# Linear attention and a GELU layer: k and v of the first batches in longer runs, the first y with t outer, and q transposed by DMA

## The chip, the cores and the metric

The kernel runs on one core of one Trainium2 chip. Time is device time of one execution in microseconds (us); the kernel before has a median of 308.79 us over three runs (308.36 to 309.51). Engines are named as in the profile: PE (TensorE, matrix multiply), DVE (VectorE), ACT (ScalarE), POOL (GpSimd) and SP (SyncE, which here only issues DMAs). SBUF is the memory that engines and DMAs share, PSUM the one that PE writes.

## The reference

Two stages. Attention takes q, k, v of 8 batches x 8 heads x 576 positions x 64. The second stage is a two-layer perceptron over 4608 tokens of width 512, with 2048 hidden columns.

```python
q_s = exp(q - max(q, axis=-1));  q_s = q_s / (sum(q_s, axis=-1) + 1e-09)   # over the 64 features
k_s = exp(k - max(k, axis=2));   k_s = k_s / (sum(k_s, axis=2) + 1e-09)    # over the 576 positions
kv  = einsum('bhsd,bhse->bhde', k_s, v)
att = einsum('bhsd,bhde->bhse', q_s, kv)
x = att.transpose(0, 2, 1, 3).reshape(4608, 512)
h = x @ w_in                                   # 512 -> 2048
y = (0.5 * h * (1 + erf(h / sqrt(2)))) @ w_out # 2048 -> 512
```

All inputs and the output are 32-bit floats. Neither kernel subtracts the maxima, which the quotients do not need. The sum over positions does not depend on their order, so k and v may be laid on the partitions in any way in which they agree; the rows of q fix which output row is which.

## The kernel before, in words

Work goes in nine chunks of 512 token rows: chunk b is positions 0 to 511 of batch b (partition p holds positions 4p to 4p+3, index j), and chunk 8 collects the 64 left over positions of all eight batches. For the sums over k the left over positions are used with their own batch.

The front of a chunk is this. `load` (L96) brings q, k, v of one batch by DMAs on SP: 1024 B runs for the main 512 positions, 256 B runs for the rest (`load_rest`, L91). ACT takes exp of q and k (`exp_q`, `exp_k`), DVE casts v to bf16 beside a column of ones per pair of heads (`cast_v`, L141). `norm_q` (L151) sums exp(q) over the features on DVE, takes reciprocals, and multiplies on POOL (or half on POOL and half on DVE). `kv_step` (L178) multiplies exp(k) with [v, 1] for one or two pairs of heads; the ones give the column sums, and DVE (or DVE and ACT, with `split`) scales the two 64x64 diagonal blocks into `kvbd`, a 128x128 block-diagonal matrix whose other blocks were set to zero once. `tp_step` (L202) transposes normalized exp(q) on PE, eight 128x128 blocks per half, and DVE copies the half from PSUM to `qT`. `x_step` (L220) multiplies `kvbd` with `qT` for one pair of heads and copies the product to `xT`.

Then `h_phase` (L239) runs 16 tiles t of four matmuls each (64 matmuls), with ACT taking GELU of each tile into `g`; `y_phase` (L254) runs, for each of four row groups j, 16 matmuls over t, and DVE copies the result, which SP stores. PSUM has three tiles for h, two for y and three for the front.

The order of the work is written by hand: every engine takes its instructions in the order of the program text. A dictionary passed to `h_phase` or `y_phase` says after which tile or matmul a piece of the next chunk's front is put. For chunk 0 the front stands alone ahead of everything (L338 to L347); for chunk 1 it is partly in the first y and its end, `kv_chain(1)` (L369), stands alone after it. From chunk 3 on the front is spread: exps on ACT after the last GELU of an h phase, `dve_front` (normalization, casts of v) in the second row of the y phase, kv, transposes and x inside the next h phase (`back`, L391: kv after tiles 1 and 2, transposes after 4 and 5, x after 8 to 11).

The weights come as 32-bit floats through five staging tiles (`wst`), and are cast to bf16: the first part of w_in by ACT (L348), the rest by DVE. In SP's order stand the loads of batch 0, five parts of w_in, four of w_out, then batches 1 and 2. A load into a staging tile waits for the cast that frees the tile, and everything after it on SP waits with it.

`warm` (L325) issues matmuls on zeros; their product is not used.

Of the kernel before, what the change touches and what calls it, by code (L numbers as in the profile page):

```python
# [11 lines left out]
ALU = mybir.AluOpType  # L12
# [4 lines left out]
def kernel(  # L17
# [11 lines left out]

    nc = tc.nc  # L30
# [10 lines left out]
    PA = 2 * D + 2  # L41

# [19 lines left out]
    v_aug = [singles.tile([128, J, HP, PA], BF16, name=f"v_aug{i}") for i in range(2)]  # L62
# [5 lines left out]
    def setup_tiles():  # L68
        nc.vector.memset(scr, 0.0)  # L69
        for i in range(2):  # L70
            nc.vector.memset(v_aug[i][:, :, :, D:D + 1], 1.0)
            nc.vector.memset(vr_aug[i][0:R, :, D:D + 1], 1.0)
            nc.vector.memset(vr_aug[i][R:128], 0.0)
            nc.vector.memset(ek_r[i][R:128], 0.0)
        for b in range(B):
            nc.gpsimd.memset(kvbd[b], 0.0)
# [6 lines left out]
    def load_main(b, name, t, eng, parts=1):  # L83
        f = f32in.tile([128, H, J * D], FP32, tag=name + "f")
# [3 lines left out]
        for i in range(parts):  # L88
            eng.dma_start(out=f[:, i * n:(i + 1) * n, :], in_=src[:, i * n:(i + 1) * n, :])

    def load_rest(b, name, t, eng):  # L91
        r = f32in.tile([R, H, D], FP32, tag=name + "r")
        st[b][name + "r"] = r
        eng.dma_start(out=r, in_=t[b, :, M:S, :].rearrange("h p d -> p h d"))

    def load(b, qp=1, kp=1, vp=1, keng=None):  # L96
        keng = keng or nc.sync
        load_main(b, "q", q, nc.sync, qp)
        load_rest(b, "k", k, keng)
        load_main(b, "k", k, keng, kp)  # L100
        load_rest(b, "v", v, nc.sync)
        load_main(b, "v", v, nc.sync, vp)

    def load_qrest():
        f = f32in.tile([128, J, H, D], FP32, tag="qf")
# [7 lines left out]
    def exp_main(b, name, parts=1):  # L113
        e = attn_sb.tile([128, J, H, D], BF16, tag="e" + name)
# [18 lines left out]

    def cast_vr(b):
# [11 lines left out]
    def cast_v_all(b):  # L146
        cast_vr(b)
        for hp in range(HP):
            cast_v(b, hp)

    def norm_q(b, parts=1, engs=None):  # L151
        engs = engs or [nc.gpsimd]
        eq = st[b]["eq"]
        qsum = small.tile([128, J, H], FP32, tag="qsum")
        recq = small.tile([128, J, H], FP32, tag="recq")
        n = H // parts
        for i in range(parts):
            hs = slice(i * n, (i + 1) * n)
            nc.vector.reduce_sum(out=qsum[:, :, hs], in_=eq[:, :, hs, :], axis=AX.X)  # L159
            nc.vector.reciprocal(recq[:, :, hs], qsum[:, :, hs])  # L160
            engs[i % len(engs)].tensor_tensor(  # L161
                out=eq[:, :, hs, :], in0=eq[:, :, hs, :],
                in1=recq[:, :, hs].unsqueeze(3).to_broadcast([128, J, n, D]), op=ALU.mult,
            )
# [13 lines left out]
    def kv_step(b, hps, split=False):  # L178
# [8 lines left out]
        for hh in range(2):  # L187
# [3 lines left out]
            if split and hh == 1:  # L191
                for i in range(n):
                    nc.scalar.activation(  # L193
                        out=dst[:, i], in_=src[:, i], func=AF.Copy, scale=rec[pr, i:i + 1]
                    )
            else:
                nc.vector.tensor_tensor(  # L197
                    out=dst, in0=src, in1=rec[pr, 0:n].unsqueeze(2).to_broadcast([64, n, D]),
                    op=ALU.mult,
                )  # L200

    def tp_step(b, half, eng="v"):  # L202
        if half == 0:
            st[b]["qT"] = attn_sb.tile([128, J, HP, 128], BF16, tag="qT", name="qT")
        ps = psum_a.tile([128, J, 2, 128], BF16, tag="a")
        for i in range(2):
# [7 lines left out]
        o = st[b]["qT"][:, :, 2 * half:2 * half + 2, :]  # L214
        if eng == "v":
            nc.vector.tensor_copy(out=o, in_=ps)  # L216
        else:
            nc.scalar.copy(out=o, in_=ps)

    def x_step(b, hp, eng="v"):  # L220
        if hp == 0:
            st[b]["xT"] = attn_sb.tile([128, HP, M], BF16, tag="xT", name="xT")
        ps = psum_a.tile([128, M], FP32, tag="a")
        if b < B:
            nc.tensor.matmul(ps, kvbd[b][:, hp, :], st[b]["qT"][:, :, hp, :], start=True, stop=True)  # L225
        else:
            for bb in range(B):
# [5 lines left out]
                )  # L233
        if eng == "v":
# [4 lines left out]
    def h_phase(c, ins):  # L239
# [3 lines left out]
        for t in range(NDF):  # L243
            ps = psum_h.tile([128, M], FP32, tag="h")
            for dm in range(NDM):
                nc.tensor.matmul(  # L246
                    ps, wi_bf[:, dm, t * 128:(t + 1) * 128], xT[:, dm, :],
                    start=(dm == 0), stop=(dm == NDM - 1),
                )
            nc.scalar.activation(out=g[:, t, :], in_=ps, func=AF.Gelu)  # L250
            for f in ins.get(t, []):
                f()

    def y_phase(c, ins):  # L254
        g = st[c]["g"]
        for j in range(J):
            ps = psum_y.tile([128, DM], FP32, tag="y")
            for t in range(NDF):
                nc.tensor.matmul(  # L259
                    ps, g[:, t, j * 128:(j + 1) * 128], wo_bf[:, t, :],  # L260
                    start=(t == 0), stop=(t == NDF - 1),
                )
                for f in ins.get((j, t), []):
                    f()
            y_sb = moe_sb.tile([128, DM], FP32, tag="y_sb")
            nc.vector.tensor_copy(out=y_sb, in_=ps)  # L266
            if c < B:
                dst = out[c * S:c * S + M, :].rearrange("(p j) n -> p j n", j=J)[:, j, :]
                nc.sync.dma_start(out=dst, in_=y_sb)
            else:  # L270
                for b2 in range(2):
# [183 lines left out]
```

The softmax here doesn't subtract the row's maximum and nothing guards it: scores larger than these inputs give would overflow.

## Time and profile before

The profiled execution took 309.37 us, its span (first to last instruction) 307.6 us.

| what | us | of the span |
|---|---|---|
| PE busy | 288.6 | 94% |
| ACT busy | 151.7 | 49% |
| DVE busy | 122.0 | 40% |
| POOL busy | 38.3 | 12% |
| chain that ended last, on PE | | 89% |
| DMA moved | 46.38 MB | 151 GB/s mean |

"Busy" counts the time from an instruction's start to its end on its engine. Matmuls follow each other in a pipeline, and the recorded length of one (386 ns for a matmul of 512 columns in the h phases) is more than the distance to the next; the distance between starts is what the chain shows. The slices of the page are 7.69 us each. The chain of waits is followed back from the last instruction: what it names at a time is what the end waited for. A DMA issue is the SP instruction; its landing comes later. Granted clock is the share of its full clock that PE was given.

### The profile page before, as it was taken

What the parts mean: (1) busy time and instruction counts of PE and PEld (TensorE: products, weight loads), DVE (VectorE), ACT (ScalarE), POOL (GpSimd) and SP (SyncE); (2) the same over time, 40 slices, a digit from 0 to 9 for tenths busy, and PEclk for the clock granted to TensorE, in tenths of its full rate; (3) what the DMA queues carried; (4) which work ended last, traced back from release to release, by engine and by line L of the source; (5) the groups of instructions that cost most, each with busy time, mean ns of one, the idle gap of its engine ahead of it and who ended that gap; (6) DMA issues with size and microseconds to landing.
All of it is one profiled execution on the core that took longest, in us unless ns stands there. A gap on an engine that the chain in (4) does not pass through costs nothing.

```text
span 307.6 us, 3824 instructions
## 1 busy us (share of the span) xinstructions
PE 288.6 (94%) x1541; PEld 138.4 (45%) x1541; DVE 122.0 (40%) x218; ACT 151.7 (49%) x212; POOL 38.3 (12%) x23
## 2 busy tenths in 40 slices
PE   5759998699899999999999999999999999999993
PEld 1424444244445544544454445444644455444441
DVE  4754437410777355342534344434433223110021
ACT  4546754367924582458245924591457056006400
POOL 6200002000204206000600060006000400000000
PEclk9588999699999999999999999999999999999999
DMA  7999999995026902691279117911600100110033
GB/s 219 316 381 387 369 263 304 312 304 152 2 102 190 286 23 84 188 271 51 73 207 270 37 69 213 265 36 68 153 21 34 70 34 0 36 70 33 2 68 68
DMA packets 47809, 46.38 MB, mean 151 GB/s; under 512 B 14000, under 2 KB 39600, under 8 KB 47792
## 3 DMA queue, kind: packets, MB, share of 16 engines
q1 hardware_dynamic: 47792, 46.14, 51.4%
q8 instruction: 12, 0.20, 0.3%
q14 instruction: 5, 0.04, 0.0%
HBM read 36.70 MB, written 9.44 MB: 150 GB/s over the span
## 4 chain that ended last, share of the span: by engine, by line
PE 89%; DVE 4%; ACT 3%; DMA 2%; issue 1%; POOL 1%; SPq 0%; ACTq 0%; DVEq 0%
PE ps L246 42%; PE ps L259 38%; PE ps L209 3%; PE ps L169 3%; PE ps L225 2%; DMA f<-in_q_dram 2%; ACT e L123 1%; DVE qsum L159 1%; PE ps L328 1%; DVE y_sb L266 1%; POOL e L161 1%; DVE xT L235 1%; PE ps L173 1%; DVE kvbd L197 0%; ACT L123 0%
## 5 line engine op out<-in xcount | busy, mean ns | idle before, releaser
L250 ACT ACTIVATE g<-ps 128x512 bf16<-128x512 f32 x144 | 86.0, 597 | 116.1 <-PE ps L246 116.1
L246 PE MATMUL ps<-xT,wi_bf 128*128 128x512 bf16 x576 | 136.5, 386 | 1.7 <-ACT wi_bf L294 1.7
L259 PE MATMUL ps<-wo_bf,g 128*128 128x512 bf16 x576 | 126.6, 379 | 1.2 <-DVE y_sb L266 1.2
L259 PEld LDWEIGHTS <-g 128*128 128x128 bf16 x576 | 56.3, 98 | 68.8 <-issue 1.9
L246 PEld LDWEIGHTS <-wi_bf 128*128 128x128 bf16 x576 | 55.9, 99 | 66.2 <-issue 4.7
L266 DVE COPY y_sb<-ps 128x512 f32<-128x512 f32 x36 | 24.8, 689 | 96.9 <-PE ps L259 96.9
L161 POOL TENSOR_TENSOR e<-e,recq 128x2048 bf16<-128x2048 bf16 (+1 forms) x9 | 33.9, 3765 | 203.8 <-DVE recq L160 171.4
L123 ACT ACTIVATE e<-f 128x2048 bf16<-128x2048 f32 (+1 forms) x20 | 31.2, 1563 | 7.9 <-DMA f<-in_q_dram 4.3
L235 DVE CAST xT<-ps 128x512 bf16<-128x512 f32 x32 | 21.8, 689 | 20.1 <-PE ps L225 16.8
L159 DVE TENSOR_REDUCE qsum<-e 128x16 f32<-128x1024 bf16 (+1 forms) x12 | 20.9, 1743 | 19.1 <-ACT e L123 18.9
L216 DVE COPY qT<-ps 128x1024 bf16<-128x1024 bf16 x17 | 11.6, 690 | 15.3 <-PE ps L209 15.3
L169 PE MATMUL ps<-v_aug,e 128*128 128x129 bf16 x128 | 11.7, 228 | 4.6 <-DVE v_aug L144 2.8
L209 PE MATMUL ps<-identity,e 128*128 128x128 bf16 x144 | 11.7, 229 | 4.0 <-POOL e L161 3.9
L169 PEld LDWEIGHTS <-e 128*128 128x128 bf16 x128 | 9.5, 101 | 9.9 <-DVE v_aug L144 2.6
L209 PEld LDWEIGHTS <-e 128*128 128x128 bf16 x144 | 9.9, 102 | 8.5 <-POOL e L161 5.0
L225 PE MATMUL ps<-qT,kvbd 128*128 128x512 bf16 x32 | 12.2, 401 | 1.5 <-ACT kvbd L193 1.2
L144 DVE CAST v_aug<-f 128x512 bf16<-128x512 f32 x32 | 11.7, 415 | 2.5 <-DMA f<-in_v_dram 2.5
L79 ACT ACT_TABLE_LOAD x9 | 11.5, 1283 | 0.9 <-PEq L439 0.7
L328 PE MATMUL ps<-zeros 128*128 128x512 bf16 x21 | 7.9, 528 | 1.2 <-DVE scr L69 1.2
L186 DVE RECIPROCAL rec<-ps 128x2 f32<-128x2 f32 (+1 forms) x18 | 3.0, 169 | 14.6 <-PE ps L173 14.6
L197 DVE TENSOR_TENSOR kvbd<-ps,rec 64x128 bf16<-64x128 f32 (+1 forms) x30 | 8.4, 278 | 0.9
L123 ACT ACT_TABLE_LOAD x6 | 7.7, 1283 | 0.1
(32 smaller groups left out, 63.1 us busy)
## 6 DMA issues: line engine op xcount, KB each, us to landing
out_dram<-y_sb SPq DMA_DIRECT2D x32, 256.0 KB, 2.3
f<-in_q_dram SPq DMA_DIRECT2D x6, 1024.0 KB, 7.5
f<-in_k_dram SPq DMA_DIRECT2D x6, 1024.0 KB, 10.5
f<-in_v_dram SPq DMA_DIRECT2D x6, 1024.0 KB, 10.2
w<-in_moe_w_out_dram SPq DMA_DIRECT2D x4, 1024.0 KB, 11.4
w<-in_moe_w_in_dram SPq DMA_DIRECT2D x3, 1024.0 KB, 11.1
f<-in_q_dram SPq DMA_DIRECT2D x4, 512.0 KB, 9.2
f<-in_k_dram SPq DMA_DIRECT2D x4, 512.0 KB, 8.9
```

The lines of the kernel that those rows point to most:

```text
L123: nc.scalar.activation(out=dst[:, i * n:(i + 1) * n], in_=src[:, i * n:(i + 1) * n], func=AF.Exp)
L144: nc.vector.tensor_copy(out=o[:, :, :, 0:D], in_=s[:, hp])
L159: nc.vector.reduce_sum(out=qsum[:, :, hs], in_=eq[:, :, hs, :], axis=AX.X)
L161: engs[i % len(engs)].tensor_tensor(out=eq[:, :, hs, :], in0=eq[:, :, hs, :], in1=recq[:, :, hs].unsqueeze(3).to_broadcast([128, J, n, D]) ...
L169: nc.tensor.matmul(ps, st[b]["ek"][:, j, hs, :].rearrange("p h d -> p (h d)"), v_aug[b % 2][:, j, hp, 0:PW], start=(j == 0), stop=False,)
L209: nc.tensor.transpose(ps[:, j, i, :], st[b]["eq"][:, j, 2 * hp:2 * hp + 2, :].rearrange("p h d -> p (h d)"), identity,)
L225: nc.tensor.matmul(ps, kvbd[b][:, hp, :], st[b]["qT"][:, :, hp, :], start=True, stop=True)
L235: nc.vector.tensor_copy(out=st[b]["xT"][:, hp, :], in_=ps)
L246: nc.tensor.matmul(ps, wi_bf[:, dm, t * 128:(t + 1) * 128], xT[:, dm, :], start=(dm == 0), stop=(dm == NDM - 1),)
L250: nc.scalar.activation(out=g[:, t, :], in_=ps, func=AF.Gelu)
L259: nc.tensor.matmul(ps, g[:, t, j * 128:(j + 1) * 128], wo_bf[:, t, :], start=(t == 0), stop=(t == NDF - 1),)
L266: nc.vector.tensor_copy(out=y_sb, in_=ps)
```

## The change

- **Loads of batches 0 and 1.** `load_pair` reads k and v of two heads as 128 rows of nine consecutive positions: runs of 2304 B, with no part for the left over positions. Each partition then belongs to one head, so `exp_k_pair` writes exp(k) block-diagonally: partitions 0 to 63 into columns 0 to 63, 64 to 127 into columns 64 to 127, the rest zero from the start. `kv_pair` sums nine matmuls of 65 columns for one pair of heads; `norm_pair` scales its two blocks. exp(k) is now in two fixed tiles instead of pool tiles, shared with the later batches. `cast_v_all` renews the ones of `v_aug` for batches 2 and 3.
- **Front of batch 0.** The second half of q is normalized on POOL instead of DVE, two casts of v and the first two of w_in are on POOL, and kv, scaling and x go pair by pair. 24 warm-up matmuls instead of 12. The zeros that they use are `kvbd[7]`. The GELU table is loaded after the first scaling.
- **h of chunks 0 and 1.** The first two tiles are interleaved (`group=2`), so that each of the four parts of xT serves two matmuls before the next is needed.
- **First y.** t is the outer loop for 12 of 16 tiles, over four PSUM tiles (two borrowed from h); then the four rows take t 12 to 15 one after another, with the transposes and the first kv of batch 1 between them. On SP q of batch 1 stands ahead of the last part of w_out. The copies of the third and fourth row are behind the rest of the front of batch 1.
- **Second y.** The two halves of the normalization of batch 2 stand on either side of the first copy; kv, transposes and x are at other places of the rows.
- **q of batches 4 to 8** (8 is the chunk of left over positions). `norm_q` stays on POOL; `xbar_step` issues one DMA on SP, written after the first matmul of the y phase's fourth row (j = 3), that writes the transpose of all of exp(q) to `qT`. `back` has transposes on PE only for batch 3.
- **The end.** The last y copy is split over DVE and ACT, and the last of its two stores leaves from ACT's queue.

```diff
+    def load_pair(b, name, t, parts):
+        f = f32in.tile([128, 2560], FP32, tag=name + "f")
+        f = f[:, 0:HP * NS * D].rearrange("p (x f) -> p x f", x=HP)
+        st[b][name + "f"] = f
+        src = t[b].rearrange("h (p n) d -> (h p) (n d)", n=NS).rearrange("(x q) f -> q x f", q=128)
+        n = HP // parts
+        for i in range(parts):
+            nc.sync.dma_start(out=f[:, i * n:(i + 1) * n, :], in_=src[:, i * n:(i + 1) * n, :])
...
+    def exp_k_pair(b, half):
+        src = st[b]["kf"].rearrange("p x (n d) -> p x n d", n=NS)
+        for hh in range(2):
+            pr = slice(hh * 64, hh * 64 + 64)
+            nc.scalar.activation(
+                out=ek_pair[half][pr, :, :, hh * 64:hh * 64 + 64],
+                in_=src[pr, 2 * half:2 * half + 2], func=AF.Exp,
+            )
...
+    def kv_pair(b, hp):
+        ps = psum_a.tile([128, 512], FP32, tag="a")
+        st[b][f"kvp{hp}"] = ps
+        for n in range(NS):
+            nc.tensor.matmul(
+                ps[:, 0:D + 1], ek_pair[hp // 2][:, hp % 2, n, :], v_pair[b][:, hp, n, 0:D + 1],
+                start=(n == 0), stop=(n == NS - 1),
+            )
...
+    def xbar_step(b):
+        st[b]["qT"] = attn_sb.tile([128, J, HP, 128], BF16, tag="qT", name="qT")
+        nc.sync.dma_start_transpose(
+            out=st[b]["qT"].rearrange("p j x m -> p (j x) m"),
+            in_=st[b]["eq"].rearrange("p j h d -> p (j h d)"),
+        )
...
-    load(0, qp=2, kp=2, vp=4)
+    load_main(0, "q", q, 2)
+    load_pair(0, "k", k, 2)
+    load_pair(0, "v", v, 4)
     wi = [load_wi(i) for i in range(5)]
-    wo = [load_wo(i) for i in range(4)]
-    load(1, qp=2, kp=2, vp=4)
+    wo = [load_wo(i) for i in range(3)]
+    load_main(1, "q", q, 2)
+    wo.append(load_wo(3))
+    load_pair(1, "k", k, 2)
+    load_pair(1, "v", v, 4)
...
+    exp_k_pair(0, 0)
+    exp_k_pair(0, 1)
+    norm_q(0, 0, 2)
+    norm_q(0, 1, 2)
+    tp_step(0, 0)
+    cast_v_pair(0, 0, nc.vector)
+    cast_v_pair(0, 1, nc.gpsimd)
+    kv_pair(0, 0)
+    tp_mm(0, 1)
+    norm_pair(0, 0, "s")
     table(AF.Gelu)
...
-    cast_wi(0, wi[0], "s")
-    cast_wi(1, wi[1], "v")
+    cast_wi(0, wi[0], "p")
+    cast_wi(1, wi[1], "p")
     cast_wi(2, wi[2], "v")
...
+    for t in range(12):
+        for j in range(J):
+            y_mm(0, yps[j], j, t)
+    norm_q(1, 0, 2)
+    norm_q(1, 1, 2)
     cast_wo(3, wo[3])
+    tp_step(1, 0)
+    for t in range(12, NDF):
+        y_mm(0, yps[0], 0, t)
+    y_out(0, yps[0], 0)
+    for t in range(12, NDF):
+        y_mm(0, yps[1], 1, t)
+    tp_step(1, 1)
+    y_out(0, yps[1], 1)
+    for t in range(12, NDF):
+        y_mm(0, yps[2], 2, t)
+    cast_v_pair(1, 0, nc.gpsimd)
+    cast_v_pair(1, 1, nc.vector)
+    kv_pair(1, 0)
+    norm_pair(1, 0, "v")
+    for t in range(12, NDF):
+        y_mm(0, yps[3], 3, t)
+    kv_pair(1, 1)
+    x_step(1, 0)
...
+    y_out(0, yps[2], 2)
+    y_out(0, yps[3], 3)
-    h_phase(1, {12: [lambda: cast_v_all(2)]})
+    h_phase(1, {12: [lambda: cast_v_all(2)]}, group=2)
...
-        s[4 + d] = [lambda: tp_step(b, 0)]
-        s[5 + d] = [lambda: tp_step(b, 1)]
+        if b < 4:
+            s[4 + d] = [lambda: tp_step(b, 0)]
+            s[5 + d] = [lambda: tp_step(b, 1)]
...
-            yi[(1, 15)] = [lambda nb=nb: dve_front(nb)]
+            yi[(1, 0)] = [lambda nb=nb: norm_q(nb)]
+            if nb < B:
+                yi[(1, 15)] = [lambda nb=nb: cast_v_all(nb)]
+            yi[(3, 0)] = [lambda nb=nb: xbar_step(nb)]
```

## The prediction

> **What bounds the kernel now.** I read the page first (engines, slices, chain), then a table of stretches, then the stretches in order of time. The page:
>
> ```profile
> span 307.6 us, 3824 instructions
> ...
> PE 288.6 (94%) x1541; PEld 138.4 (45%) x1541; DVE 122.0 (40%) x218; ACT 151.7 (49%) x212; POOL 38.3 (12%) x23
> ...
> PE   5759998699899999999999999999999999999993
> ...
> PEclk9588999699999999999999999999999999999999
> DMA  7999999995026902691279117911600100110033
> ...
> PE 89%; DVE 4%; ACT 3%; DMA 2%; issue 1%; POOL 1%; SPq 0%; ACTq 0%; DVEq 0%
> ```
>
> From the twelfth slice (7.69 us each) PE is full and at full clock: what shortens the kernel there is fewer PE instructions. Only the first eleven slices have holes, and there the DMA engines are busy without a break to the tenth. The stretches, cut where PE changes stage (columns: time, length, busy time and instructions of PE, its weight loads, DVE, ACT, POOL; granted clock, DMA share, GB/s):
>
> ```profile
> core 0: us, PE busy (x) PEld busy (x) DVE busy (x) ACT busy (x) POOL busy (x), PEclk, DMA share, GB/s
> 0.00:21.20 21.20, 12.35 (x61) 6.04 (x61) 12.75 (x32) 11.17 (x16) 6.33 (x15) 0.84 0.97 298
> ...
> 36.90:59.10 22.20, 18.38 (x106) 8.82 (x104) 13.42 (x25) 10.83 (x15) 1.90 (x1) 0.92 1.13 288
> ...
> 74.40:93.10 18.70, 17.19 (x107) 8.82 (x105) 11.65 (x20) 11.72 (x10) 1.90 (x1) 1.00 0.12 44
> ...
> 154.20:170.90 16.70, 16.70 (x105) 8.66 (x104) 6.34 (x13) 8.96 (x15) 0.00 (x0) 1.00 0.80 220
> ```
>
> 154.20 to 170.90 is a steady h phase: 64 matmuls (13.82 us, 216 ns each) and 2.88 us of attention work, no idle time. The first three rows are the front, first y and second y, each with time in which PE waits. The chain names it (start, length, what):
>
> ```profile
> 20.14 1.05 ACT wi_bf L294
> 21.24 15.67 PE ps L246 x64
> ...
> 52.45 0.33 DVE vr_aug L136
> ...
> 58.18 0.32 ACT kvbd L193
> ...
> 59.15 15.49 PE ps L246 x64
> ...
> 160.96 0.45 PE ps L209 x8
> ```
>
> The first h matmul waits for xT of batch 0 and then for a 1.05 us weight cast queued behind it on ACT. Between 51.76 (last matmul of the first y) and 59.15 the front of batch 1 runs alone, DVE and ACT in turn. In the steady part eight transposes cost PE 0.45 us, with nothing to hide them.
>
> **Part 1, k and v in 2304 B runs.** Arrivals are read where an engine waits for its DMA. The second half of q lands at 6.37, the second of k at 11.02 (ACT starts): 1.18 MB in 4.65 us. The weights, 2048 B runs, come at 23.22, 25.93, 28.64 (DVE starts): 1.05 MB in 2.71 us. At that rate k takes 3.05; the new runs are a little longer, so I take 3.05; bounds 3.05 and 4.65. From 11.02 to 20.51 v and the first three weight parts land: 9.49 - 2.71 - 2 x 1.69 (as the two q halves, 4.68 to 6.37) = 3.4 for v, so 0.35 less. About 2 us per batch; batch 0's k lands at 7.9 and 9.4, v at 10.2 to 12.5, the weight parts at 14.0, 15.5, 18.2, 20.9, 23.6, wo at 26.3, 29.0, 32.0, q of batch 1 by 35.5, wo[3] (now behind it) at 38.2, k by 41.3, v by 44.3. SP holds these back only where a wo load waits for a staging tile; POOL has freed the first by about 16.
>
> **Part 2, the front of batch 0.** exp(k) becomes four ACT instructions of 64x1152. 128x1024 takes 1.06 us and 128x2048 1.91, 0.83 ns an element, so 1.17 each, 4.7 against 2.74 before (0.63 + 2 x 1.06): they run 7.9 to 12.6. The second q half is now normalized on POOL behind the first (1.90 each, to 11.3; DVE ended at 10.41), so its transposes start 0.9 later. kv is 9 matmuls of 65 columns per pair against 5 of 129; at the 57 ns of the kv rows (0.23 for four) 0.51 against 0.28, all in PE holes. Per pair then follow, in series, the cast, matmuls, reciprocal (0.17), two scalings (0.22 DVE, 0.31 ACT) and x with its copy (0.59 to 0.69). Walking the written order: pair 0 scaled at 12.9, Gelu table (1.28 + 0.20) to 14.4, pair 1 at 14.7, pair 2 at 15.0, pair 3 at 16.05, last x 16.05 to 16.3. The weight cast is no longer behind it: POOL does the first part, landed at 14.0. A POOL cast is not in the trace; bounds are DVE's 0.67 for 128x1024 and the POOL multiply, 1.90 with two inputs. I take 1.9, nearest by engine: done at 15.9, second part 17.8, needed at 18.0. With two h tiles interleaved, the eight matmuls wait little for the last xT (17.05). First h matmul 16.3 against 21.24: **-4.9** (bounds -2.5, where POOL and DVE hold each other up as the 2048-element multiply does, 4.91 beside DVE casts against 3.62 alone, and -6.5). DVE's new memsets of exp(k)'s zeros (four of 576 words, about 0.6 each by the 0.27 for 256) end near 5.1, covered by DVE's wait for q to 5.77; the 24 warm-up matmuls (8 at 0.43 until the granted clock rises at 4.4, then 0.22) end at 8.1, covered by PE's wait to 9.39. Without that cover each would push the whole front by its overrun.
>
> **Part 3, first y and front of batch 1.** The first h took 15.67, not 13.82, at a granted clock of 0.50 to 24.84; I keep it: y starts at 32.0. wo casts (DVE, 1.23) end by 27.5, 30.3, 33.2, the third needed at 38.9; 48 matmuls to 42.4, transposes, four quarter rows of y between them, kv of pair 0 (k, v landed by 41.3 and 42.8) to 47.2. Then remains a DVE chain: cast of pair 1, then four reciprocals, eight scalings, one cast, one x copy, to 51.15; x of pair 3; h at 51.5. From h to h this is 35.2 against 37.91: **-2.7** (bounds 0, and -6 if the half clock of the first and second h goes). The y copies moved behind this chain (two, 0.69) delay two SP stores and load(3) behind them; their data is due only at 73, where q of batch 3 is read, and lands near 62.
>
> **Part 4, second y.** It took 18.49 (74.67 to 93.16); its own work is 13.82 + 2.88. PE stood from 81.9 to 83.83 for a y copy that DVE had behind two q normalizations. The second normalization is now behind the first y copy, and kv is asked for at matmul 13 of the second row, 6.25 after the start; exp(k) ends at 6.5. Stall 0.25: 17.0, **-1.5** (bounds 0 and -1.8).
>
> **Part 5, transposes by DMA.** Five times 16 transposes leave PE: 5 x 2 x 0.45 = **-4.5**; the ten DVE copies (0.69) were hidden. The DMA needs the normalized q:
>
> ```profile
> 147.51 4.91 POOL L161 TENSOR_TENSOR e<-e,recq 128x2048 bf16<-128x2048 bf16 x1 [25.67 <-DVE recq L160]
> ...
> 163.83 0.38 PE L225 MATMUL ps<-qT,kvbd 128*128 128x512 bf16 x1
> ```
>
> POOL ends at 152.42; x reads qT at 163.83, less 0.9 now: 10.5 us of cover (10.6 and 10.7 in the first and last batch). No transposing DMA is in the trace. It moves 2048 rows of 256 B, four times an r load:
>
> ```profile
> out_dram<-y_sb SPq DMA_DIRECT2D x32, 256.0 KB, 2.3
> ...
> r<-in_k_dram SPq DMA_DIRECT2D x8, 128.0 KB, 8.0
> ...
> f<-in_q_dram SPq DMA_DIRECT2D x8, 128.0 KB, 3.5
> ```
>
> With nothing ahead 128 KB of such rows land in 3.5, 256 KB of long rows in 2.3. Lower bound 2.3; upper 4 x 3.5 = 14.0, as if the quarters went one after another. In a stream the r load adds 1.46 (6.37 to 7.83), so I take 2.3 + 4 x 1.46 = 8.1: hidden. If the cover is gone each us costs 5 us in all. On SP the last y store and the next loads stand behind the wait, which ends at 152.4, before that store's data (154.9); loads issued at 155.4 land within 15 and are read from 172 on, so a few us to spare.
>
> [...]
>
> **Part 6, the end.** The last copy (302.87, 0.69) is halved over DVE and ACT and the two stores leave from two queues; the last issue ended at 304.70, now near 303.7: **-0.9** (bounds -0.4, -1.05).
>
> **Sum.** -4.9 - 2.7 - 1.5 - 4.5 - 0.9 = -14.5. The profiled execution took 309.37 (1.8 around its span): 294.9. The median of the runs is 308.79, 0.58 lower: 294.3.
>
> **Rivals.** (a) The front is not shortened: POOL's casts are slow or hold DVE up, its chain merely moves. For: DVE and ACT both have chains of some 5 us per front, and POOL stretches from 3.62 to 4.91 beside DVE. Against: ACT's 1.05 us cast and the 7.4 us hole are plainly taken apart. By the weak bounds -2.5, 0, 0, -4.5, -0.4 = -7.4: 301.4. (b) Slower: the DMA transpose takes more than the cover. At 14.0 it is 3.5 late five times, +17.5: 311.8. It decides from 10.5 + 14.5/5 = 13.4 us on. Against: 512 KB in 14 us is 37 GB/s, where 256 B rows went at 90 (131 KB in 1.46). (c) Between, a transpose of 11 to 13 us: 297 to 307. (d) The change does not do what it says: 2304 B runs are no faster. Then arrivals come some 2 us later per batch, the front loses about that: 296.3, inside the likeliest case's range.
>
> **How the numbers follow.** Likeliest with (d) 0.68, own range 288 (all strong bounds 288.9, less the 0.4 by which the fastest run is under the median) to 302; (a) 0.17; (b) 0.10; (c) 0.05. Range 288 to 303 leaves (b), (c) and a little out. This kernel's measurement tells about 0.5% from no change. Faster 0.68 + 0.17 + 0.02 of (c) = 0.87; within 0.5% 0.02; slower 0.11.
>
> **What would show it.** Part 2: first h matmul near 16. Part 3: second h near 51. Part 4: no PE hole before the second row's copy. Part 5: h phases of 15.8 instead of 16.7 in the steady part, a DMA landing under 10 us after POOL, no PE wait before x. The forecast fails where x waits for qT, where the first h waits for a POOL cast, or where PE waits for DMA between 30 and 50.

## The result, and the profile after

The changed kernel takes **318.11 us** (median of four runs, 314.64 to 318.66) against 308.69 us (308.36 to 309.51) of the kernel before: a ratio of 1.028, with a 95% interval of 1.020 to 1.036. It is slower. The forecast was 294.3 us with a range of 288 to 303, so it missed by 23.8 us and on the wrong side.

The profiled execution took 318.66 us. Its page, first the same parts that were shown of before:

```profile
span 316.9 us, 3738 instructions
...
PE 291.0 (92%) x1498; PEld 135.8 (43%) x1498; DVE 133.2 (42%) x214; ACT 152.8 (48%) x210; POOL 42.7 (13%) x32
...
PE   8599997999959997999699969996999999999994
...
PEclk9979996899997997999899999999899999999999
DMA  7999999990198006790379209930660150010022
...
PE 75%; DVE 18%; ACT 2%; issue 2%; DMA 1%; POOL 1%; DVEq 0%; ACTq 0%; POOLq 0%
```

PE has 43 instructions fewer and yet more busy time (291.0 against 288.6), since more of it ran at a lower clock (mean granted clock 0.962 against 0.972). The slices, now 7.9 us each, show where: the steady part, which was full from the twelfth slice on, has holes at slices 12, 16, 20, 24 and 28, and in the chain DVE has grown from 4% to 18%. From the 29th slice to the last but one nothing is missing.

Phase starts make that exact. The first h or y matmul of each phase, and the length to the next phase's first, in us:

| phase | before | forecast | after |
|---|---|---|---|
| h of chunk 0 (start) | 21.2 | 16.3 | 17.4 |
| h of chunk 1 (start) | 58.9 | 51.5 | 53.0 |
| second y (length) | 18.5 | 17.0 | 16.9 |
| h of chunk 2 (length) | 16.7 | 16.7 | **22.1** |
| y of chunks 2, 3, 4, 5 (length) | 13.8 each | 13.8 each | **18.1, 18.2, 16.4, 18.1** |
| h of chunks 3 to 6 (length) | 16.7 each | 15.8 each | 15.8 each |
| y of chunks 6 and 7 (length) | 13.8 each | 13.8 each | 13.8 each |
| last y to the end | 18.7 | 17.8 | 18.5 |

Up to the h phase of chunk 2 the kernel is 7.1 us ahead of before (85.9 against 93.0). Then one h phase loses 5.4 and four y phases lose 4.3 + 4.4 + 2.6 + 4.3 = 15.6, together 21.0 us. The stretches of the changed kernel, cut at its phases (columns as in the table of before):

```profile
core 0: us, PE busy (x) PEld busy (x) DVE busy (x) ACT busy (x) POOL busy (x), PEclk, DMA share, GB/s
...
17.40:53.00 35.60, 33.33 (x185) 15.58 (x184) 19.74 (x31) 20.14 (x27) 6.08 (x4) 0.93 1.07 355
...
85.90:108.00 22.10, 18.42 (x105) 9.69 (x104) 13.76 (x21) 8.96 (x15) 3.98 (x1) 0.92 0.63 167
...
126.20:142.00 15.80, 15.80 (x90) 7.79 (x89) 4.95 (x11) 8.96 (x15) 0.00 (x0) 1.00 0.93 240
142.00:160.20 18.20, 15.66 (x66) 6.63 (x65) 9.71 (x10) 7.60 (x7) 3.91 (x1) 0.91 0.29 74
...
176.00:192.40 16.40, 13.94 (x65) 6.26 (x64) 9.71 (x10) 7.60 (x7) 3.94 (x1) 1.00 0.22 67
```

The h phase of 126.2 is what the forecast said: 15.80 us, no idle time. The y phase of 142.0 has the same 64 matmuls as before, 2.5 us in which PE stands, and a mean granted clock of 0.91. PE's waits in the changed kernel name who it stood for (total, times, longest):

```profile
PE ps L340 <- DVE y_sb L352: 10.0, 4, 2.5
PE ps L237 <- DVE v_aug L210: 3.7, 1, 3.7
```

The timeline of one such y phase, after (start, length, engine, line, operation; in brackets the idle time ahead and what ended it):

```profile
149.28 3.91 POOL L229 TENSOR_TENSOR e<-e,recq 128x2048 bf16<-128x2048 bf16 x1 [30.10 <-DVE recq L228]
149.30 5.09 DVE L210 CAST v_aug<-f 128x512 bf16<-128x512 f32 x4
...
154.31 1.28 DVE L352 COPY y_sb<-ps 128x512 f32<-128x512 f32 x2
155.05 5.30 PE L340 MATMUL ps<-wo_bf,g 128*128 128x512 bf16 x16 [2.54 <-DVE y_sb L352]
...
156.05 2.12 SPq L289 DMA_TRANSPOSE qT<-e  x1
```

and of the same y phase before:

```profile
147.51 4.91 POOL L161 TENSOR_TENSOR e<-e,recq 128x2048 bf16<-128x2048 bf16 x1 [25.67 <-DVE recq L160]
147.54 1.42 DVE L144 CAST v_aug<-f 128x512 bf16<-128x512 f32 x4
...
148.87 0.68 DVE L266 COPY y_sb<-ps 128x512 f32<-128x512 f32 x1
```

The same four casts of v took 1.42 us beside POOL's multiply and now take 5.09; the multiply itself is shorter, 3.91 instead of 4.91. The chain of the changed kernel splits the casts:

```profile
149.38 0.34 DVE v_aug L210
149.72 0.02 issue
149.75 3.73 DVE v_aug L210
153.48 0.02 issue
153.50 0.44 DVE v_aug L210
...
154.31 0.69 DVE y_sb L352
```

One cast of the four takes 3.73 us, and it ends 0.3 us after POOL's multiply (149.28 + 3.91 = 153.19). Behind it stands the y copy of row 1; row 3 needs that row's PSUM tile, of which y has two; so PE stands for 2.54 us. The 16 matmuls that follow take 5.30 us; from the first of them to the next phase's first matmul it is 5.14 us, where a row at full clock takes 3.45. In the y phases of chunks 6 and 7, where no v is left to cast, nothing of this is seen.

### The profile page after: what moved, and what is told of

Its sections match the earlier page's. It is cut to its first block, busy times and chain, and to the rows that moved or that the text cites. A ratio compares the mean times of both kernels' runs of the same rounds, so it can differ in the third digit from the quotient of the medians.

```text
span 316.9 us, 3738 instructions
## 1 busy us (share of the span) xinstructions
PE 291.0 (92%) x1498; PEld 135.8 (43%) x1498; DVE 133.2 (42%) x214; ACT 152.8 (48%) x210; POOL 42.7 (13%) x32
## 4 chain that ended last, share of the span: by engine, by line
PE 75%; DVE 18%; ACT 2%; issue 2%; DMA 1%; POOL 1%; DVEq 0%; ACTq 0%; POOLq 0%
PE ps L330 39%; PE ps L340 30%; DVE v_aug L210 7%; DVE qsum L227 4%; PE ps L303 2%; DVE y_sb L352 2%; PE ps L237 2%; DMA f<-in_q_dram 1%; PE ps L272 1%; DVE kvbd L198 1%; DVE v_aug L174 1%; ACT e L152 1%; DVE qT L279 1%; POOL e L229 1%; ACT ek L152 1%
## 5 line engine op out<-in xcount | busy, mean ns | idle before, releaser
L340 PE MATMUL ps<-wo_bf,g 128*128 128x512 bf16 x576 | 133.2, 389 | 10.0 <-DVE y_sb L352 10.0
L316 DVE CAST xT<-ps 128x512 bf16<-128x512 f32 x32 | 22.1, 690 | 36.4 <-PE ps L303 27.8
L210 DVE CAST v_aug<-f 128x512 bf16<-128x512 f32 x24 | 26.7, 1112 | 2.2 <-DMA f<-in_v_dram 1.6
L152 ACT ACTIVATE e<-f 128x1024 bf16<-128x1024 f32 (+1 forms) x11 | 15.8, 1442 | 3.3 <-DMA f<-in_q_dram 3.2
L237 PE MATMUL ps<-v_aug,ek 128*128 128x129 bf16 x96 | 9.0, 231 | 3.7 <-DVE v_aug L210 3.7
L168 ACT ACTIVATE ek<-f 64x1152 bf16<-64x1152 f32 x8 | 9.3, 1162 | 4.6 <-DMA f<-in_k_dram 4.5
L152 ACT ACTIVATE ek<-f 128x2048 bf16<-128x2048 f32 x6 | 11.4, 1894 | 0.0
L237 PEld LDWEIGHTS <-ek 128*128 128x128 bf16 x96 | 7.5, 104 | 7.3 <-issue 4.4
L408 PE MATMUL ps<-kvbd 128*128 128x512 bf16 x26 | 8.4, 491 | 1.2 <-DVE scr L82 1.2
L279 DVE COPY qT<-ps 128x1024 bf16<-128x1024 bf16 x8 | 5.5, 689 | 7.2 <-PE ps L272 7.0
L259 DVE TENSOR_TENSOR kvbd<-ps,rec 64x128 bf16<-64x128 f32 x24 | 6.9, 289 | 0.6
## 6 DMA issues: line engine op xcount, KB each, us to landing
w<-in_moe_w_out_dram SPq DMA_DIRECT2D x4, 1024.0 KB, 12.6
```

The lines of the kernel that those rows point to most:

```text
L152: nc.scalar.activation(out=dst[:, i * n:(i + 1) * n], in_=src[:, i * n:(i + 1) * n], func=AF.Exp)
L210: nc.vector.tensor_copy(out=o[:, :, :, 0:D], in_=s[:, hp])
L237: nc.tensor.matmul(ps, st[b]["ek"][:, j, hs, :].rearrange("p h d -> p (h d)"), v_aug[b % 2][:, j, hp, 0:PW], start=(j == 0), stop=False,)
L316: nc.vector.tensor_copy(out=st[b]["xT"][:, hp, :], in_=ps)
L340: nc.tensor.matmul(ps, st[c]["g"][:, t, j * 128:(j + 1) * 128], wo_bf[:, t, :], start=(t == 0), stop=(t == NDF - 1),)
```

## The theory and its rivals

What is different for those casts is a part of the diff that the forecast passed over. `v_aug` is now a view of a flat tile that `v_pair` shares, and in the trace the second, third and fourth cast of a batch each carry a wait on the semaphore that the cast before raises; in the kernel before they carry no wait, though they write the same places of `v_aug`.

**Theory A.** The wait leaves DVE a moment without an instruction between two casts. In it POOL's multiply, already issued, starts in earnest, and the next cast stands until the multiply is over. The y copy is late, PE stands, its clock drops.

**Theory B.** The transposing DMA, new in just these phases and issued there, holds the y phase up: it moves rows of 256 B out of the tile and into another, and the stores of y stand behind it on SP.

**Theory C**, on the size alone: the lower clock in row 3 comes from the load and not from the hole.

## Experiments

### The view alone, put into the kernel before

```diff
-    v_aug = [singles.tile([128, J, HP, PA], BF16, name=f"v_aug{i}") for i in range(2)]
+    v_flat = [singles.tile([128, HP * 9 * 66], BF16, name=f"v_aug{i}") for i in range(2)]
+    v_aug = [
+        t[:, 0:J * HP * PA].rearrange("p (j x w) -> p j x w", j=J, x=HP) for t in v_flat
+    ]
```

> The kernel before with one edit: v_aug is a view of a flat tile of the changed kernel's size, so that each cast of v waits for the one before. No transposing DMA, no other part of the change. Theory A: the same holes appear, y phases 4 x (2.5 to 4.3) and the third h phase 2 to 5: 320 to 331, with a second cast of v of over 3 us in each y phase. Theory B: as before, 308 to 310.

Measured: **329.19 us** (326.71 to 329.85), ratio 1.063 (1.057 to 1.070). Nothing else of the change is in this kernel, and it is 20 us slower than the kernel before. Its h phase of chunk 2 takes 22.1 us, its y phases of chunks 2 to 5 take 16.4, 18.0, 16.5 and 18.2: 5.4 + 13.9 us more than before, which is nearly the whole loss (its span is 19.5 us longer). The same place in its timeline:

```profile
155.84 3.91 POOL L164 TENSOR_TENSOR e<-e,recq 128x2048 bf16<-128x2048 bf16 x1 [29.30 <-DVE recq L163]
155.87 5.09 DVE L147 CAST v_aug<-f 128x512 bf16<-128x512 f32 x4
...
160.87 1.28 DVE L269 COPY y_sb<-ps 128x512 f32<-128x512 f32 x2
161.61 5.11 PE L262 MATMUL ps<-wo_bf,g 128*128 128x512 bf16 x16 [2.54 <-DVE y_sb L269]
```

There is no transposing DMA in it. B falls as the cause.

### The transposes back on PE, the view kept

```diff
-        if b < 4:
-            s[4 + d] = [lambda: tp_step(b, 0)]
-            s[5 + d] = [lambda: tp_step(b, 1)]
+        s[4 + d] = [lambda: tp_step(b, 0)]
+        s[5 + d] = [lambda: tp_step(b, 1)]
...
-            yi[(3, 0)] = [lambda nb=nb: xbar_step(nb)]
```

> The changed kernel with the transposes of q of batches 4 to 8 back on PE, as before; the casts of v as changed. Theory A: the holes stay and the transposes cost 5 x 0.9 again, 319 to 324. Theory B: the holes go and the transposes come back, about 300 to 304.

Measured: **321.62 us** (320.33 to 322.88), ratio 1.040 (1.035 to 1.046). The y phases of chunks 2 to 5 take 18.1, 18.2, 17.9 and 16.5 us without any DMA in them, and the h phases are back at 16.7. Taking the DMA away cost time.

### The waits taken away: a tile of its own for each pair of heads

```diff
-    small = ctx.enter_context(tc.tile_pool(name="small", bufs=4))
+    small = ctx.enter_context(tc.tile_pool(name="small", bufs=3))
...
-    v_flat = [singles.tile([128, HP * NS * VW], BF16, name=f"v_aug{i}") for i in range(2)]
+    v_flat = [
+        [singles.tile([128, NS * VW], BF16, name=f"v_aug{i}_{x}") for x in range(HP)]
+        for i in range(2)
+    ]
```

(`small` gives up one buffer to make room; the uses of `v_aug` and `v_pair` index the list of tiles.)

> The changed kernel with the v tile of each pair of heads as a tile of its own (and the small pool with 3 buffers for 4, for space), so that from batch 4 on a cast of v no longer waits for the cast before it. Theory A (those waits leave a gap in which POOL's multiply takes what DVE needs, and the second cast stands some 3.4 us): the four y phases of chunks 2 to 5 lose the hole of 2.5 us and most of the half clock after it, 4 x (2.5 + 1.8) = 17 at most; batches 2 and 3 still wait for the ones written just before, so the hole in the third h phase stays. About 301 to 305. Theory B (the transposing DMA, new in these y phases, is what holds them): no change, 315 to 319.

Measured: **296.32 us** (295.67 to 296.74), ratio 0.958 (0.955 to 0.962), better than A's figure and 2.0 us from the forecast of 294.3. All y phases from chunk 2 on take 13.8 us and the h phase of chunk 2 takes 16.7: the hole of batch 3, which A had left in, went too: its casts still carry a wait each, but find it met, and also run in one piece (one starts every 0.33 us).

### The waits kept, the casts ahead of the normalization

Here every cast still waits for the one before, but POOL's multiply is asked for only behind them.

```diff
     def dve_front(b):
-        norm_q(b)
         if b < B:
             cast_v_all(b)
+        norm_q(b)
...
-                yi[(1, 15)] = [lambda nb=nb: cast_v_all(nb)]
+                yi[(1, 0)].insert(0, lambda nb=nb: cast_v_all(nb))
```

> The changed kernel with the casts of v ahead of the normalization of q from batch 3 on; the waits between the casts stay. Theory A with its second half (it takes POOL's multiply running beside the casts): the casts take about 0.4 us each, the holes go, in the third h phase too: 294 to 299. If the waits alone cost the time, the casts stay slow and it stays at 314 to 319. Theory B: 314 to 319.

Measured: **295.94 us** (295.30 to 296.46), ratio 0.957 (0.954 to 0.961). So a wait between casts by itself costs PE next to nothing, and POOL beside casts without waits costs next to nothing (the experiment before); it takes both. (The h phase of chunk 2 is 17.4 us here, with 0.5 us in which PE waits for the multiply that now comes later.) This run leaves every tile of the changed kernel, and all four buffers of `small`, as they are, so neither the places of the tiles nor that buffer is the cause. The casts of batches 3 to 7, one at a time (least, median and greatest ns, first and last start), in the changed kernel:

```profile
L210 DVE CAST v_aug<-f x20: 408/428/3727, 89.8 to 220.2; 128x512 bf16<-128x512 f32 x20
```

with tiles of their own:

```profile
L212 DVE CAST v_aug<-f x20: 407/415/418, 87.0 to 197.1; 128x512 bf16<-128x512 f32 x20
```

and with the casts first:

```profile
L210 DVE CAST v_aug<-f x20: 415/428/433, 84.3 to 195.3; 128x512 bf16<-128x512 f32 x20
```

Where POOL is out of the way the waits make a cast 13 ns longer (428 against 415), and as a cast then starts only when the one before is done, the distance from one to the next is 0.46 us instead of 0.33. Where POOL is not, they cost 3.3 us once a batch. POOL's multiply shows the same trade from the other side: alone it takes 3.62 us, in this last kernel always; with casts in one piece beside it 4.91 (before) or 4.92 to 5.03 (own tiles), which is 3.62 and most of the 1.42 us of the casts; with casts that wait 3.91 to 3.98, which is 3.62 and most of one cast. By these lengths the casts and the multiply take turns. That is not so of every cast: in the front of the changed kernel a DVE cast of 128x576 starts at 10.59, 0.5 us before POOL's multiply ends, and takes 0.75 us, as long as its like with POOL idle.

That a wait between two DVE instructions is enough for the turn to pass, the runs show by themselves: beside the multiply a cast behind such a wait takes up to 3.73 us and ends 0.3 us after the multiply, and none that follows without a pause takes more than 0.42. Why the two take turns they do not show.

### Both cures together

The casts first in the y phases, on the version with own tiles.

```diff
-                yi[(1, 15)] = [lambda nb=nb: cast_v_all(nb)]
+                yi[(1, 0)].insert(0, lambda nb=nb: cast_v_all(nb))
```

> The version with own v tiles (296.32 us), and in the y phases also the casts of v ahead of the normalization of q. If either cure alone takes the whole hole away, the two together change nothing: 295.3 to 297.0, y phases of 13.8 us, with POOL's multiply at 3.6 instead of 4.9 us. If some of the hole was left, 294 to 295.

Measured: **295.24 us** (294.91 to 297.34), ratio 0.957 (0.953 to 0.961). As expected, either cure takes the whole hole away; the three times overlap. The multiply is at 3.62 us again. These versions beat both kernels by 12 us or more.

### Filling the hole: how much of it is the clock

```diff
+    def fill(n):
+        ps = psum_a.tile([128, DM], FP32, tag="a")
+        for i in range(n):
+            nc.tensor.matmul(ps, zeros[:, 0:128], zeros, start=True, stop=True)
...
         for j in range(J):
+            if j == 3 and 2 <= c <= 5:
+                fill(10)
             ps = psum_y.tile([128, DM], FP32, tag="y")
```

> The changed kernel as it is, with ten matmuls on a tile of zeros (2.1 us) ahead of row 3 in the y phases of chunks 2 to 5, where PE stood for 2.5 us. The casts of v still stand behind POOL's multiply and row 3 starts as late as before. If the lower clock of row 3 (16 matmuls in 5.30 us instead of 3.45) is the answer to that hole, row 3 takes 3.45 to 3.6 us in all four and the sum is 5.5 us less than the changed kernel's 318.1: 312.6, or 309.5 where the first two h phases also get the full clock, as they did in the run of 314.64. If the lower clock comes from something else (the load, the time since the last such stretch), row 3 still takes 5.3 us in three of four and the time stays at 314.6 to 318.5.

Measured: **312.52 us** (310.64 to 314.34), ratio 1.012 (1.006 to 1.018), 5.6 us less than the changed kernel, with more work for PE. The y phases of chunks 2 to 5 take 16.4 to 16.5 us. One of them:

```profile
148.29 5.10 DVE L210 CAST v_aug<-f 128x512 bf16<-128x512 f32 x4
...
151.33 2.32 PE L410 MATMUL ps<-kvbd 128*128 128x512 bf16 x10
...
153.30 1.28 DVE L352 COPY y_sb<-ps 128x512 f32<-128x512 f32 x2
154.04 3.61 PE L340 MATMUL ps<-wo_bf,g 128*128 128x512 bf16 x16 [0.38 <-DVE y_sb L352]
```

The cast is as late as ever, but row 3 takes 3.61 us instead of 5.30 (3.45 instead of 5.14 from start to start). C falls: the lower clock is the answer to the hole. Of the 21.0 us lost, row 3 starting 2.6 to 2.7 us late four times is 10.7, three rows at the lower clock, 1.6 to 1.7 us each, are 5.0, and the h phase of chunk 2 is 5.4 (3.7 of waiting and the rest at a lower clock).

### The DMA transposes by themselves

Own tiles, and q of batches 4 to 8 transposed on PE again.

```diff
-        if b < 4:
-            s[4 + d] = [lambda: tp_step(b, 0)]
-            s[5 + d] = [lambda: tp_step(b, 1)]
+        s[4 + d] = [lambda: tp_step(b, 0)]
+        s[5 + d] = [lambda: tp_step(b, 1)]
...
-            yi[(3, 0)] = [lambda nb=nb: xbar_step(nb)]
```

> The changed kernel with own v tiles for each head pair, and q of batches 4 to 8 transposed on TensorE again: one step, the DMA transposes, is undone on the good version (296.32 us). If the transposes by DMA are worth what TensorE no longer does (2 x 0.45 us in each of five h phases, 15.8 back to 16.7), the time is 300.8 us (300.3 to 301.6). If they were worth less because what PE saves comes back elsewhere (a wait for psum_a, a later x), it stays at 296 to 298. If they cost time in sum it falls below 296.

Measured: **301.17 us** (299.59 to 302.91), ratio 0.975 (0.970 to 0.981), 4.85 us above the version with the DMA. Five h phases are 0.89 us longer each, 4.5 in all. The forecast's 4.5 for this part holds.

### A transposing DMA among loads

Own tiles, and batch 3 also by DMA, where loads are in flight.

```diff
-        if b < 4:
+        if b < 3:
             s[4 + d] = [lambda: tp_step(b, 0)]
...
             ins[0] = [lambda: dve_front(3)]
+            ins[1] = [lambda: xbar_step(3)]
```

> The version with own v tiles (296.32 us), and q of batch 3 transposed by DMA too, in the h phase of chunk 2, where the loads of batch 4 are in flight (84 to 100 us) and PE needs the transposed q at 96.35 us; POOL's multiply ends at 91.9. If a transposing DMA takes 4.5 us from its issue whatever else is moved, it lands at 96.4, PE waits under 0.5 us, the h phase loses its two 0.45 us of transposes, and the time is 295.4 to 296.3. If it stands in line behind the loads issued before it, it lands after the last of them (100.2 us), PE waits 4 to 7 us in the h phase and loses another 1 to 3 to a halved clock: 300 to 306.

Measured: **303.10 us** (302.49 to 305.38), ratio 0.984 (0.979 to 0.989), 6.8 us more than with that one batch on PE.

```profile
86.25 5.02 POOL L232 TENSOR_TENSOR e<-e,recq 128x2048 bf16<-128x2048 bf16 x1 [14.03 <-DVE v_aug L217]
...
91.30 7.58 SPq L292 DMA_TRANSPOSE qT<-e  x1
...
100.95 0.59 PE L306 MATMUL ps<-qT,kvbd 128*128 128x512 bf16 x1 [5.99 <-DMA qT<-e]
```

The DMA landed at 100.90, 9.6 us after its issue began; its issue alone took 7.58 us. Of the six transposing DMAs of this run it is the slowest: the quickest landed after 4.3 us, the median is 4.5. The five loads of batch 4, issued from 83.76 to 90.02, stand ahead of it on SP, and the landing, PE's wait and the time are those of the second reading of the expectation, by which it stands in line behind them. PE waited 5.99 and the h phase took 24.9 us instead of 16.7. This is the case of the forecast's rival (b), which the change itself avoids: its five transposes go at the end of y phases, when no load is in flight ahead of them, and land 4.4 to 5.4 us after issue.

### The 2304 B runs undone

Own tiles, and k and v of batches 0 and 1 in 1024 B runs with `exp_k`, `cast_v` and the five matmuls of a pair as before.

```diff
-    load_pair(0, "k", k, 2)
-    load_pair(0, "v", v, 4)
+    load_both(0, "k", k, 2)
+    load_both(0, "v", v, 4)
...
-    exp_k_pair(0, 0)
-    exp_k_pair(0, 1)
+    exp_k(0, 2)
...
```

> The version with own v tiles (296.32 us), with k and v of batches 0 and 1 loaded, exponentiated, cast and multiplied as in the kernel before (1024 B runs, 128x1024 exponentials, five matmuls of a head pair, kv still one head pair at a time): the 2304 B runs alone are undone. If the runs are worth what they gain at arrival (k 3.05 instead of 4.65 us, v 0.35 less: 2.0 us a batch), the first h phase starts at 19 instead of 17.2 us, because its weights and the last v come 2 us later, the second 2 to 4 us later than 52.0, and the time is 298.3 to 300.5. If the longer exponentials of the runs (four of 1.18 us against 0.63 + 2 x 1.06) take back what arrives earlier, both phases start within 0.7 us of where they did and the time is 296 to 297.3.

Measured: **296.75 us** (295.21 to 297.33), ratio 0.960 (0.956 to 0.964). The times of the two versions can't be told apart. The places can: the first h phase starts at 19.0 instead of 17.2, the second at 54.1 instead of 52.0, and the second y at 67.9 instead of 66.1. Arrivals move too: k of batch 0 lands at 10.74 instead of 9.73 (1.0 us, where 1.6 was expected), the last of v at 14.62 instead of 12.75 (1.9 us, where 2.0 was). Both readings of the expectation were half right: the positions move by the 1.8 to 2.1 us of the arrivals, but of that only 1.7 is in the two spans (294.8 against 293.1) and 0.4 in the medians. Executions differ by such amounts in the first two h phases, whose granted clock is not the same each time (13.8 us at full clock; the changed kernel's profile has 15.0 and 16.0). So what the runs are worth in time, 0.4 us by the medians and 1.7 by the two profiled spans, is not settled.

### The first y in rows again

```diff
-    for t in range(12):
-        for j in range(J):
+    for j in range(J):
+        for t in range(12):
             y_mm(0, yps[j], j, t)
```

> The version with own v tiles (296.32 us), and the first 48 matmuls of the first y phase in rows again (j outer, t inner): row 0 needs the third chunk of wo after 8 matmuls (1.7 us) instead of 32, and its cast ends 3.3 us after the phase starts, so PE waits 1.5 us there. If the front of batch 1 is bound by PE, the second h phase starts 1.5 us later or, with a halved clock after the hole, 3 us later: 298 to 299.5. If it is bound by the arrival of v (last quarter at 44.9 us) and by the chain of its kv steps, 0 to 0.7 us later: 296 to 297.

Measured: **297.43 us** (296.72 to 298.63), ratio 0.964 (0.959 to 0.968). Inconclusive: in its profiled execution the first h phase started 1.1 us later than in the version it is compared with, so that PE stood for the third part of w_out for only 0.21 us instead of the 1.5 expected, and the y stretch was 20.8 us long against 21.0. What the order of the loops is worth when the front is on time is open.

### The end: two tiles for the two halves of the last copy

On the version with both cures.

```diff
         if last:
+            y_s2 = moe_sb.tile([128, DM], FP32, tag="y_sb", name="y_s2")
+            rows = out[2 * j * S:(2 * j + 2) * S, :].rearrange("(b s) n -> b s n", b=2)[:, M:S, :]
             nc.vector.tensor_copy(out=y_sb[:, 0:DM // 2], in_=ps[:, 0:DM // 2])
-            nc.scalar.copy(out=y_sb[:, DM // 2:DM], in_=ps[:, DM // 2:DM])
+            nc.sync.dma_start(out=rows[:, :, 0:DM // 2], in_=y_sb[:, 0:DM // 2])
+            nc.scalar.copy(out=y_s2[:, DM // 2:DM], in_=ps[:, DM // 2:DM])
+            nc.scalar.dma_start(out=rows[:, :, DM // 2:DM], in_=y_s2[:, DM // 2:DM])
+            return
...
```

> The version with own v tiles and the casts first (295.24 us), and the two halves of the last copy in two tiles, each stored by one DMA from its engine's queue. In the changed kernel ACT's half (0.37 us) starts only when DVE's (0.42) is done, because both write one tile. If that wait is why the end was not shortened as forecast, ACT's half now starts with DVE's, both issues leave 0.4 us earlier, and the last stretch, from the first matmul of the last y phase to the end, is 18.0 to 18.1 us instead of 18.5; the median then is 294.5 to 295.2, a difference that the medians can't settle. If the end is set by the landing of the stores alone, or 1024 B runs land later, it stays at 18.4 to 18.7.

Measured: **300.54 us** (299.52 to 302.75), ratio 0.974 (0.970 to 0.979), 5.3 us slower than without this edit. Both expectations fell.

```profile
288.11 0.42 DVE L354 COPY y_sb<-ps 128x256 f32<-128x256 f32 x1 [2.76 <-PE ps L343]
288.57 0.64 SPq L355 DMA_DIRECT2D out_dram<-y_sb  x1
288.57 0.37 ACT L356 COPY y_s<-ps 128x256 f32<-128x256 f32 x1 [13.68 <-DVE y_sb L354]
288.98 1.13 ACTq L357 DMA_DIRECT2D out_dram<-y_s  x1
```

ACT still starts only when DVE is done, now with a tile of its own to write. In the trace ACT's copy carries, here as in the changed kernel, a wait on the semaphore that DVE's copy raises, and starts 0.03 us after that copy's end, so the order looks like one that the program asks for. What the two still share is the PSUM tile that both read; whether that is the reason was not tried. And the two stores, each 128 x 256 with an outer dimension of two, crawl: their 262 KB move from 289.8 to 296.2, at 41 GB/s, where the last four 64-row stores of the version without this edit had landed 2.3 to 2.7 us after their issue.

## Why the forecast was wrong, step by step

**The step that failed** is in Part 5 and the sum: the steady part was costed as 4.5 us saved and nothing added, with the y phases at 13.8 us as before. It has no term for `v_aug`, which the change made a view of a shared tile, and so put at nothing that the four casts of a batch became a chain of waits. A wait on an instruction of the same engine looks free, and it nearly is (0.13 us a cast), until a POOL multiply waits for its turn (3.3 us a batch). The cost came to 21.0 us, 15.6 in the y phases and 5.4 in the h phase of chunk 2. No rival named it. Rival (a) had the fact it rests on, that the multiply takes 3.62 us alone and 4.91 beside DVE casts, but drew it for the front and as a cost for POOL; that the price can change sides, 3.3 us for DVE, was not seen.

**Part 1** held but for k: k of batch 0 landed at 9.82 (forecast 9.4), 3.8 us behind q instead of 3.05; v at 12.85 (12.5), 3.0 behind k as forecast; the third weight part at 18.55 (18.2). The last of v is in 1.9 us earlier than before, about the 2 us of the forecast. Rival (d) fell as to the arrivals; what they are worth in time is open.

**Part 2** gave 3.9 of 4.9 us: first h at 17.4, not 16.3. POOL's casts of the weights took 1.18 us a part (two of 0.59), not the 1.9 taken; the first part was ready at 15.6 and not on the path. What was under-sized is the chain of x. It begins 0.5 us late, with k: the exponentials end at 13.08 instead of 12.6, and the Gelu table is loaded at 14.9 instead of 14.4. And the idle time of PE ahead of its steps (1.13 and 0.76 us ahead of the x matmuls of pairs 1 and 3, both for ACT's scaling) was left out of the sum.

**Part 3** was forecast at 35.2 us from h to h and took 35.7, but not in its parts: the h phase was 0.7 us shorter than taken, and from y to the next h it was 1.1 us longer. The DVE chain at its end was under-sized: its eight scalings took 0.29 us each, not the 0.22 read in the kernel before, and a cast of a pair 0.75.

**Part 4**: 17.0 forecast, 16.9 measured; PE waited nowhere in that y for a copy. The forecast misread the wait in the kernel before, though: PE stood for the copy only from 82.67 to 83.83, and ran kv matmuls until then. The rest of the 1.8 us lay in shorter waits, among them 0.35 us ahead of the last x matmul; the sum came out because it took the phase as a whole.

**Part 5's** gain came in full: h phases of 15.8, and 4.85 us in the run with PE transposes. The landing was over-sized, 8.1 taken against 4.4 to 5.4 in the trace, inside bounds of 2.3 and 14.0; rivals (b) and (c) fell for this change, and the run among loads shows the condition under which they would not have. At the 4.4 us the 0.5 MB go at 119 GB/s, the issue of 2.2 us included.

**Part 6** gave 0.2 of 0.9 us: the halves of the last copy run one after the other (0.42 on DVE, then 0.37 on ACT), where the sum had them side by side. The last issue leaves 0.37 us sooner after the start of the phase than before, and the store from ACT's queue lands 2.62 us after its issue, where the last one from SP had taken 2.39.

Added up from the forecast's 294.9: 1.0 (Part 2), 0.5 (Part 3), 0.5 for the second h phase (16.0 instead of 15.5), -0.1 (Part 4), 21.0 (the casts), 0.7 (Part 6) make 318.5; the execution took 318.66. Without the 21.0 the forecast would have been off by 2.6 us, and the versions that take them away measured 295.2 to 296.3.

That these come so near 294.3 is in part luck. In the profile of the version with own tiles the first two h phases took 13.8 and 14.1 us at nearly full clock, 3.3 us less in sum than the 15.7 and 15.5 that the forecast kept, and that made up for what Parts 2, 3 and 6 fell short.

## What to carry to other kernels

When tiles are merged or turned into views, read the new waits in the instruction streams, those of an engine on itself too, and ask for each who may slip into the pause: here a DVE cast that waits for its predecessor lets a 3.6 us POOL multiply in ahead of it. In this kernel either of two ways was enough: put short DVE work ahead of the instruction that starts long POOL work, or keep it in one piece without waits. A hole of 2.5 us in the stream of matmuls cost up to 4.4 here: row 3 started 2.7 us late, and ran 1.7 us longer at the lower clock.

## What was not expected of the hardware

- A DVE cast of 0.42 us took 3.73 us beside a POOL multiply once a pause of 0.04 us stood ahead of it, while four casts in one piece pushed the multiply back instead (4.91 us for 3.62). Which of the two was stretched was decided by the pause, not by which is asked for first: in the kernel before, in the changed one and in that with own tiles, the multiply and the first cast start within 0.13 us of each other, the multiply first.
- A hole of 2.5 us was enough for the lower clock in three of four y phases of the changed kernel (5.1 us for the 16 matmuls of row 3, from start to start, instead of 3.45), in two of four of the kernel before with the view, and in three of four with the transposes back on PE. Its length did not decide: in the changed kernel 2.47 us was enough at 118.6, and 2.46 us was not at 186.5. In the clock records of the kernel before and of the changed one every change falls on a grid of 3.41 us. In the y phases of the changed kernel the clock fell to 0.50, for one step, where the step before held 2.13 to 2.42 us of the hole (falls at 122.19, 156.33 and 221.18), and stayed where no step held more than 1.94, so here it was the place of the hole on the grid that decided. With 0.3 to 0.4 us left of the hole, in the run with filling matmuls, row 3 took its full-clock time in all four.
- A transposing DMA of 128 x 2048 two-byte elements landed 4.4 to 5.4 us after its issue in the changed kernel, where only stores of y were in flight ahead of it, and its issue held SP for 2.1 to 3.7 us; behind loads it landed after 9.6 us and the issue took 7.58.
- Two stores of 128 x 256 floats with an outer dimension of two moved at 41 GB/s together, and cost the end 5 us. While they move the mean busy share of the 16 DMA engines is 0.1 to 0.2, that of two or three of them; in the version without this edit it is 0.7 to 0.9 in the middle of the 64-row stores. Whether the outer dimension of two is the reason was not tried.
